# Chunked attention feeding a mixer: undivided groups from the third batch's attention on, held sums, and earlier copies of q

## The chip, the cores and the metric

The kernel runs on one core of a Trainium2 chip. The metric is the device time of one execution in microseconds (us). The five engines of a core are called here TensorE (PE; its weight loads are PEld), VectorE (DVE), ScalarE (ACT), GpSimd (POOL) and SyncE (SP), which only issues DMAs.

## The reference

Two stages. The first is attention over chunks: 4 batches, 8 heads, 768 positions of 64 numbers. For each chunk of 32 queries the keys are 8 memory keys, 16 positions to the left, the chunk and 8 to the right.

```python
for c in range(nc):
    q_c = q[:, :, c_start:c_end]
    k_full = np.concatenate([mem_k, k[:, :, l_start:r_end]], axis=2)
    v_full = np.concatenate([mem_v, v[:, :, l_start:r_end]], axis=2)
    scores = scale * np.matmul(q_c, k_full.transpose(0, 1, 3, 2))
    a = np.exp(scores - np.max(scores, axis=-1, keepdims=True))
    a = a / (np.sum(a, axis=-1, keepdims=True) + 1e-09)
    out[:, :, c_start:c_end] = np.matmul(a, v_full)
```

The second stage takes the result, 768 positions of 512 numbers for each batch, as x and mixes it:

```python
h = x.transpose(0, 2, 1) @ U @ V
u = x + h.transpose(0, 2, 1)
out = u + np.maximum(u @ w_ch1, 0.0) @ w_ch2      # 512 -> 2048 -> 512
```

All is float32 (U, V and the weights arrive as 64-bit numbers and are decoded on the chip). A number is split into a high and a low part, and each product is made of three matmuls (high by high, high by low, low by high).

## The kernel before, in words

**Stages.** Attention of batch 0 comes first (to about 49 us). Then the mixer's matmuls go batch by batch, and the attention of batch b + 1 is laid piece by piece between the matmuls of batch b. Batch 0's matmuls run to about 214 us, with batch 1's attention from about 122 us; batch 1's to about 372, with batch 2's attention; batch 2's to about 528, with batch 3's attention; batch 3's to the end, alone.

**The mixer.** 768 positions are two blocks of 384. In batch 0 the two blocks are computed plainly (`w1_step`, `w2_step`). From batch 1 on `fast` multiplies both blocks and pairs of hidden tiles at once with seven products in place of eight: `fold_both` makes seven sums of transposed u (`th`, `tl`, high and low part), `prepare` makes five sums of weight tiles of a pair on GpSimd, and `build_factor` splits them into high and low on ScalarE (cast) and VectorE (subtraction). `products(p)` runs the 42 matmuls of pair p into three PSUM banks, `first_block` and `second_block` the second layer.

**Borders.** After the third and the seventh product and after every `w2_step` stands a border (`fast_border`; in batch 0 `border`). There the next item of the attention is written: a turn of k or q (transposes on TensorE, then copies by ScalarE or VectorE), a score part, a turn of the softmax's result, or a weighing part (softmax times v). `PLACES` says at which borders the 20 items stand. The third score part is at border 23, the second weighing at 24.

**Halved groups.** A score part (`s_part`) and a weighing part (`av_part`) have 128 small matmuls each (64 rows by 32 columns, 64 numbers) into two PSUM banks. The first 64 (`half(0)`) are written at the item's border. The second 64, and the softmax or the result's scaling behind them, go into the list `tails`, which is run at the start of the next border.

**Order.** TensorE, GpSimd and SyncE issue in the order in which the program is written, all through. VectorE does so until unit 18 of batch 0 (about 129 us), ScalarE until unit 2. After that a planner orders ScalarE and VectorE from modelled times and priorities; work written under `tc.high_priority(offset=HIGH)` goes ahead of what was written up to 400 steps earlier. PSUM has five banks for the running work (`ps_b`) and three for accumulators (`ps_o`); in SBUF 19 equal slots hold what comes and goes.

**Lines that matter.** L661 score matmuls, L784 weighing matmuls, L681 and L682 maximum and subtraction of the softmax, L582 a turn, L642 the copies of turned q, L600 an edge copy of turned k, L1336 GpSimd's sums, L1417 and L1418 the two steps of `build_factor`, L1379 the fold's sums, L1384 its low parts, L1167 the addition to x, L1206 and L1211 the second layer, L1449 the products. `turned[0][1]` is `tl`; its element (4, 0, last column) is written by the last low part of the last fold.

Of the kernel before, what the change touches and what calls it, by code (L numbers as in the profile page):

```python
# [9 lines left out]
F32 = mybir.dt.float32  # L10
# [26 lines left out]
HIGH = 400  # L37
# [18 lines left out]
def chunk_attn_then_mixer_kernel(  # L56
# [13 lines left out]
    nc = tc.nc  # L70
    ctx.enter_context(tc.manual_schedule(engines={mybir.EngineType.SP}))
    P = 128
# [18 lines left out]
    TOK = TB * P  # L91
# [3 lines left out]
    const = ctx.enter_context(tc.tile_pool(name="const", bufs=1))  # L95
# [73 lines left out]
    for j in range(4):  # L169
        nc.gpsimd.tensor_copy(  # L170
            out=rep[32 * j:32 * j + 32],
            in_=ident[32 * j:32 * j + 32, None, 32 * j:32 * j + 32].broadcast_to([32, 3, 32]),
# [252 lines left out]
    def attention(b, xs):  # L425
# [207 lines left out]
        def q_part(T, h, copy=nc.scalar.copy):  # L633
            psv = turn(qn.pop((T, h)))
            if front[0]:
                qt = home([P, 2, NB, CK], F32, "qt", f"w1_{5 + (2 * T + h) % 3}")
            else:
                qt = slot([P, 2, NB, CK], F32, "qt")
            qts[T, h] = qt
            for q_ in range(2):  # L640
                to, src = qt[:, q_].rearrange("c i (n r) -> c r i n", r=2), psv[:, q_]
                copy(out=to, in_=src)  # L642
# [89 lines left out]
        def s_recip(T):  # L732
# [2 lines left out]
            nc.vector.tensor_scalar_add(out=rs, in0=rs, scalar1=1e-9)  # L735
            nc.vector.reciprocal(out=rs, in_=rs)

        def s_part(T):
            banks, psv, half = s_half(T)

            def others():
                half(1)
                s_weights(T, banks, psv)
                s_sums(T)
                s_recip(T)

            tails.append(others)

        def t_part(T, s):
            pt = pts[T, s]  # L750
# [8 lines left out]
        def av_part(T):  # L759
            psv, half = av_half(T)  # L760

            def others():
                half(1)
                x_part(T, psv)
                issued.add(f"av{T}")

            tails.append(others)

        def av_turn(T):
            psv, half = av_half(T)  # L770
# [195 lines left out]
        else:  # L966
# [27 lines left out]
                part(T, h)  # L994

            def q_shared(T, h):
                q_part(T, h, (nc.scalar.copy, nc.vector.tensor_copy)[h])

            order = (
                (turn_in, (k_part, "kn", 0)), (turn_in, (q_shared, "qn", 0)), (turn_both, (1,)),  # L1000
# [303 lines left out]
    tails = []  # L1304
# [6 lines left out]
    def border():  # L1311
        run_tails()
        place(PLAN[at[0]])
        at[0] += 1

    sums_d = [[dram.tile([P, 2, 2, P], F32, name=f"sumsd{p}_{m}") for m in range(3)] for p in range(NF // 2)]

    def prepare(p, first):

        if first:  # L1320
            whole = [slot([P, NCK, P], F32, "val") for _ in range(2)]
            for side in range(2):
                nc.gpsimd.dma_start(out=whole[side], in_=val_d[2 * p + side])
            mixed[p, 1], mixed[p, 3] = whole[1][:, 2:4, :], whole[0][:, 0:2, :]
        else:
            plain = slot([P, 2, 2, P], F32, "plain")
        for m, (n, fa, ca, fb, cb, op) in enumerate(SUMS):
            if m % 2 == 0:
                two = slot([P, 2, 2, P], F32, "sums")
                used = slice(0, 1 if m + 1 == len(SUMS) else 2)  # L1330
                if not first:
                    nc.sync.dma_start(out=two[:, used], in_=sums_d[p][m // 2][:, used])
            mixed[p, n] = two[:, m % 2]
            if first:
                a, b_ = (whole[f][:, 2 * c:2 * c + 2, :] for f, c in ((fa, ca), (fb, cb)))
                nc.gpsimd.tensor_tensor(out=two[:, m % 2], in0=a, in1=b_, op=getattr(ALU, op))  # L1336
                if m % 2 == 1 or m + 1 == len(SUMS):
                    summed.append((p, sums_d[p][m // 2][:, used], two[:, used]))
            elif m == 0:
                for n, side in ((1, 1), (3, 0)):  # L1340
                    mixed[p, n] = plain[:, side]
                    nc.sync.dma_start(out=plain[:, side], in_=val_d[2 * p + side][:, 2 * side:2 * side + 2])
# [244 lines left out]
```

## Time and profile before

| | |
|---|---|
| time, median of 3 runs | 659.44 us (659.01 to 659.98) |
| profiled execution, its own time | 656.65 us |
| its span, first to last instruction | 654.9 us |
| mean granted clock of TensorE | 0.992 |
| PE | 629.9 us busy (96%), 6198 matmuls |
| PEld | 548.8 us (84%), 6198 weight loads |
| DVE | 419.6 us (64%), 889 instructions |
| ACT | 306.9 us (47%), 770 instructions |
| POOL | 74.2 us (11%), 128 instructions |
| DMA | 96.83 MB in 134357 packets, mean 148 GB/s |

The profile is of one execution. Busy time counts an engine's instructions; a wait is the idle time before an instruction and is put down to what ended it. "issue" means that nothing in the profile ended it. Matmuls are pipelined, so that a busy matmul may be shown longer than the step to the next one. A granted clock of 1.00 is 2.4 GHz, 0.50 is 1.2 GHz.

### The profile page before, as it was taken

Reading aid. Unit: us, or ns where it says so; the run is one execution under the profiler, and the core shown is the slowest. Engines: PE = TensorE matmul, PEld = TensorE weight load, DVE = VectorE, ACT = ScalarE, POOL = GpSimd, SP = SyncE. Lnnn points to the kernel's source line nnn. Section 1 sums busy time; section 2 is a strip of 40 time slices with the busy share of each in tenths; the row PEclk is TensorE's granted clock in tenths of the full one; section 3 lists DMA queues with packets and bytes.
Section 4 is the critical chain, followed back from the end, with each engine's and each line's share of the span. In section 5 each row is a group of like instructions: output and inputs, shape, how many; then the busy total and the mean of one; then the engine's idle time right before and its main releaser. Section 6 shows DMA issues by size and latency. Waiting matters only on the chain.

```text
span 654.9 us, 15747 instructions
## 1 busy us (share of the span) xinstructions
PE 629.9 (96%) x6198; PEld 548.8 (84%) x6198; DVE 419.6 (64%) x889; ACT 306.9 (47%) x770; POOL 74.2 (11%) x128
## 2 busy tenths in 40 slices
PE   8788999999999899998999999998999999999997
PEld 6667999978878898777898899877979899989986
DVE  4877997886539756347576863655756975427442
ACT  4566676585226455324334555632433643315321
POOL 3610011100112630123300000000000000000000
PEclk9899999999999999998999999999999999999999
DMA  8797685695606888133361689143422673101022
GB/s 209 180 302 285 216 268 167 195 272 138 186 18 217 226 211 239 33 99 108 104 233 49 170 206 235 34 114 107 130 86 92 206 237 97 49 6 43 2 70 76
DMA packets 134357, 96.83 MB, mean 148 GB/s; under 512 B 88842, under 2 KB 111114, under 8 KB 134282
## 3 DMA queue, kind: packets, MB, share of 16 engines
q1 hardware_dynamic: 121690, 70.25, 38.8%
q10 hardware_dynamic: 9936, 17.04, 7.0%
q0 software_dynamic: 2656, 8.52, 3.9%
q8 instruction: 49, 0.80, 0.5%
q14 instruction: 26, 0.21, 0.1%
HBM read 69.44 MB, written 25.43 MB: 145 GB/s over the span
## 4 chain that ended last, share of the span: by engine, by line
PE 88%; DMA 5%; DVE 3%; SPq 1%; issue 1%; ACT 1%; DVEq 0%; ACTq 0%
PE ps_h L1449 20%; PE acc L1206 14%; PE ps_h L1152 9%; PE ps_a L1449 8%; PE acc L1211 7%; PE ps_h L1206 6%; PE ps_a L1206 5%; PE ps_h L1211 3%; PE ps_a L582 2%; PE ps_a L1211 2%; PE ps_a L784 2%; DMA rw<-in_moe_w_ch_dram 2%; PE ps_a L661 2%; DMA vb<-in_v_dram 2%; PE ps_a L754 1%; PE ps_h L1198 1%
## 5 line engine op out<-in xcount | busy, mean ns | idle before, releaser
L1206 PE MATMUL acc<-w,hh 128*128 128x512 f32 x366 | 97.5, 401 | 1.0 <-DVE w L367 1.0
L1449 PE MATMUL ps_h<-th,w1l 128*128 128x384 f32 x288 | 84.5, 345 | 0.0
L1206 PEld LDWEIGHTS acc<-w,hh 128*128 128x128 f32 x366 | 66.7, 188 | 15.4 <-issue 1.5
L1425 DVE SCALAR_TENSOR_TENSOR hl<-kept,hh 128x384 fp32r<-128x384 f32 x48 | 26.9, 561 | 55.4 <-PE ps_a L1211 29.0
L1424 ACT ACTIVATE hh<-kept 128x384 fp32r<-128x384 f32 x48 | 25.4, 530 | 67.1 <-PE ps_a L1206 42.6
L1449 PEld LDWEIGHTS ps_h<-th,w1l 128*128 128x128 f32 x288 | 53.4, 190 | 3.2 <-issue 1.7
L1449 PE MATMUL ps_h<-th,s 128*128 128x384 f32 x192 | 52.9, 336 | 0.0
L1211 PE MATMUL acc<-w,hl 128*128 128x512 f32 x183 | 51.7, 390 | 0.0
L1449 PE MATMUL ps_h<-tl,w1l 128*128 128x384 f32 x144 | 48.9, 340 | 1.2 <-DVE tl L1384 1.2
L1206 PE MATMUL ps_h<-w,hh 128*128 128x512 f32 x156 | 43.5, 401 | 0.0
L1152 PE MATMUL ps_h<-uh,w1h 128*128 128x384 f32 x124 | 42.2, 346 | 0.8 <-ACT uh L1124 0.8
L1152 PE MATMUL ps_h<-ul,w1h 128*128 128x384 f32 x124 | 40.8, 337 | 0.0
L1211 PEld LDWEIGHTS acc<-w,hl 128*128 128x128 f32 x183 | 34.4, 188 | 7.5
L1206 PE MATMUL ps_a<-w,hh 128*128 128x512 f32 x132 | 37.9, 390 | 1.8 <-ACT hh L1158 1.8
L1455 ACT COPY part<-ps_h 128x384 f32<-128x384 f32 x24 | 11.5, 480 | 58.5 <-PE ps_h L1449 48.0
L1457 DVE TENSOR_TENSOR part<-ps_a,part 128x384 f32<-128x384 f32 x24 | 13.3, 556 | 35.8 <-PE ps_a L1449 34.6
L1417 ACT CAST s<-sums 128x256 fp32r<-128x256 f32 x72 | 28.6, 412 | 15.2 <-PE ps_h L1449 15.2
L1449 PEld LDWEIGHTS ps_h<-th,s 128*128 128x128 f32 x192 | 35.1, 188 | 0.0
L1336 POOL TENSOR_TENSOR sums<-val 128x256 f32<-128x256 f32 x40 | 31.5, 812 | 25.2 <-DMA val<-vald 14.2
L1206 PEld LDWEIGHTS ps_h<-w,hh 128*128 128x128 f32 x156 | 28.1, 188 | 5.7
L1418 DVE TENSOR_TENSOR w1l<-sums,w1l 128x256 fp32r<-128x256 f32 x48 | 21.2, 442 | 18.0 <-ACT w1l L1417 17.8
L1449 PE MATMUL ps_h<-tl,s 128*128 128x384 f32 x96 | 32.3, 336 | 0.0
(279 smaller groups left out, 1414.5 us busy)
## 6 DMA issues: line engine op xcount, KB each, us to landing
sums<-sumsd SPq DMA_DIRECT2D x32, 256.0 KB
xd<-x ACTq DMA_DIRECT2D x30, 256.0 KB
x<-xd SPq DMA_DIRECT2D x30, 256.0 KB
rw<-in_moe_w_ch_dram SPq DMA_DIRECT2D x14, 512.0 KB
vb<-in_v_dram SPq DMA_DIRECT2D x56, 98.0 KB
raw<-in_moe_w_ch_dram SPq DMA_DIRECT2D x20, 256.0 KB
qn<-in_q_dram SPq DMA_DIRECT2D x36, 128.0 KB
rw<-in_moe_w_ch_dram SPq DMA_DIRECT2D x16, 256.0 KB
```

Source lines behind the costliest of these rows:

```text
L582: nc.tensor.transpose(out=psv[:, p, r, :], in_=half[:, r, 2 * p:2 * p + 2, :].rearrange("n h d -> n (h d)"), identity=ident,)
L661: nc.tensor.matmul(out=psv[s][CK * i:CK * i + CK, t, p % 2, p // 2, :], lhsT=qt[p // 2][rows, p % 2, NI * t + i, :], rhs=kall[rows, NB * ( ...
L1152: nc.tensor.matmul(out=ph[:, :TOK], lhsT=w[:, c, :], rhs=u[c], start=(m == 0), stop=(m + 1 == len(parts)),)
L1206: nc.tensor.matmul(out=acc[tt], lhsT=h[:, sl], rhs=w, start=(begins and m == 0), stop=False,)
L1211: nc.tensor.matmul(out=acc[tt], lhsT=hl[:, sl], rhs=w2h[f], start=False, stop=ends is not None)
L1336: nc.gpsimd.tensor_tensor(out=two[:, m % 2], in0=a, in1=b_, op=getattr(ALU, op))
L1417: nc.scalar.copy(out=s[:, 0:2], in_=total)
L1418: nc.vector.tensor_tensor(out=s[:, 2:4], in0=total, in1=s[:, 0:2].bitcast(F32), op=ALU.subtract)
L1424: nc.scalar.activation(out=hh, in_=src, func=AF.Relu)
L1425: nc.vector.scalar_tensor_tensor(out=hl, in0=src, scalar=0.0, in1=hh.bitcast(F32), op0=ALU.max, op1=ALU.subtract,)
L1449: nc.tensor.matmul(out=banks[at_], lhsT=w[:, wc, :], rhs=t[:, i, c, :], start=(n < 3 and m == 0), stop=(m + 1 == len(parts)), skip_group_c ...
L1457: nc.vector.tensor_tensor(out=ta, in0=b2, in1=ta, op=ALU.subtract)
```

## The change

Three edits.

1. A score part and a weighing part hand their second half to a new function, `put_off`. While batch 1's attention is written it goes into `tails` as before. For batches 2 and 3 it is run at once, so that all 128 matmuls, and the softmax or the scaling, are written at the item's own border. (Batch 0's attention does not use these functions.) "Batch 0" in the change's own name is the batch whose matmuls run beside batch 1's attention.
2. The copies of the first turned q of batch 1 (`q_shared`: two on ScalarE, two on VectorE) are written with priority.
3. GpSimd copies one number out of `tl` into a new one-column tile ahead of its five sums for the second pair of batch 1. The number is written by the last low part of the last fold, and GpSimd issues in order, so these sums, and all that is written behind them on GpSimd, come after that fold.

```diff
+        def put_off(others):
+            if b == 1:
+                tails.append(others)
+            else:
+                others()
+
         def s_part(T):
             banks, psv, half = s_half(T)
...
                 s_sums(T)
                 s_recip(T)
 
-            tails.append(others)
+            put_off(others)
...
                 x_part(T, psv)
                 issued.add(f"av{T}")
 
-            tails.append(others)
+            put_off(others)
...
             def q_shared(T, h):
-                q_part(T, h, (nc.scalar.copy, nc.vector.tensor_copy)[h])
+                with tc.high_priority(offset=HIGH):
+                    q_part(T, h, (nc.scalar.copy, nc.vector.tensor_copy)[h])
...
+    gate_ = const.tile([P, 1], F32, name="gate")
...
             mixed[p, 1], mixed[p, 3] = whole[1][:, 2:4, :], whole[0][:, 0:2, :]
+            if p == 1:
+                nc.gpsimd.tensor_copy(out=gate_[0:1], in_=turned[0][1][0:1, 4, 0, TOK - 1:TOK].bitcast(F32))
```

## Rows read from the trace of the kernel before

**Rows 1.** TensorE's waits, whole span: who waited for whom, total us, times, longest.

```profile
PE ps_a L784 <- DVE pt L682: 5.3, 4, 2.4
PE ps_a L661 <- issue: 3.9, 3, 1.7
```

**Rows 2.** Timeline, TensorE, batch 1: start us, us, instruction, idle before, releaser.

```profile
292.54 0.86 PE L661 MATMUL ps_a<-kall,qt 64*32 64x64 f32 x64
...
296.67 0.86 PE L661 MATMUL ps_a<-kall,qt 64*32 64x64 f32 x64
...
299.90 0.27 PE L784 MATMUL ps_a<-vb,pT 64*32 64x64 f32 x2 [2.37 <-DVE pt L682]
```

**Rows 3.** Timeline of the same stretch, VectorE.

```profile
297.91 1.29 DVE L681 TENSOR_REDUCE mx<-ps_a 128x8 f32<-128x512 f32 x2
299.12 1.28 DVE L682 TENSOR_TENSOR pt<-ps_a,mx 128x512 f32<-128x512 f32 x2
```

**Rows 4.** Timeline, TensorE, batch 2, the same place.

```profile
455.36 0.27 PE L784 MATMUL ps_a<-vb,pT 64*32 64x64 f32 x2 [2.32 <-DVE pt L682]
```

**Rows 5.** Three stretches: busy us of PE, PEld, DVE, ACT, POOL, granted clock, DMA.

```profile
293.40:296.70 3.30, 3.30 (x24) 3.05 (x24) 1.19 (x3) 1.19 (x3) 0.56 (x1) 1.00 0.66 250
301.20:304.60 3.40, 3.40 (x23) 3.35 (x11) 1.28 (x4) 0.78 (x2) 2.79 (x4) 0.50 0.02 5
456.70:460.10 3.40, 3.40 (x27) 3.38 (x20) 1.80 (x5) 1.57 (x4) 0.00 (x0) 1.00 0.02 5
```

**Rows 6.** Timeline, TensorE: an undivided group of the opening, a half group.

```profile
36.54 1.48 PE L784 MATMUL ps_a<-vbe,pt 64*32 64x64 f32 x128
...
271.18 0.86 PE L784 MATMUL ps_a<-vb,pT 64*32 64x64 f32 x64
```

**Rows 7.** Timeline, TensorE, second score part of batch 1's matmuls.

```profile
277.37 0.86 PE L661 MATMUL ps_a<-kall,qt 64*32 64x64 f32 x64
...
280.45 0.76 PE L661 MATMUL ps_a<-kall,qt 64*32 64x64 f32 x52
281.98 0.33 PE L661 MATMUL ps_a<-kall,qt 64*32 64x64 f32 x12 [0.77 <-issue]
```

**Rows 8.** The page's DMA queues: packets, MB, share of 16 engines.

```profile
q8 instruction: 49, 0.80, 0.5%
```

**Rows 9.** DMA packets that began from 279.4 to 279.6 us: packets, MB, share.

```profile
q8 instruction: 1, 0.02, 33.8%
```

**Rows 10.** Timeline, TensorE and ScalarE, first score part of batch 1's attention.

```profile
133.59 1.03 PE L582 MATMUL ps_a<-ident,qn 128*128 128x128 f32 x8
...
138.23 0.26 ACT L600 COPY kall<-ps_a 128x48 f32<-128x48 f32 x1
...
140.52 0.74 ACT L642 COPY qt<-ps_a 128x256 f32<-128x256 f32 x2
...
141.07 0.96 PE L661 MATMUL ps_a<-kall,qt 64*32 64x64 f32 x64 [1.37 <-issue]
```

**Rows 11.** Timeline, GpSimd, around the last fold.

```profile
209.06 4.30 POOL L1336 TENSOR_TENSOR sums<-val 128x256 f32<-128x256 f32 x5 [3.05 <-DVE tl L1384]
...
222.30 0.73 POOL L590 COPY kall<-memkT 128x256 f32<-128x256 f32 x2
```

**Rows 12.** Line 1418 from 190 to 240: duration ns minimum/median/maximum, starts.

```profile
L1418 DVE TENSOR_TENSOR s<-sums,s x9: 418/421/965, 210.0 to 236.4; 128x256 fp32r<-128x256 f32 x9
```

**Rows 13.** Timeline, VectorE, around the last fold.

```profile
210.03 2.73 DVE L1418 TENSOR_TENSOR s<-sums,s 128x256 fp32r<-128x256 f32 x3
212.68 1.73 DVE L1379 TENSOR_TENSOR fold<-ps_a,fold 128x256 f32<-128x256 f32 x5
...
215.28 1.27 DVE L1167 TENSOR_TENSOR x<-acc,x 128x512 f32<-128x512 f32 x2
```

**Rows 14.** Timeline, TensorE, start of batch 1's products.

```profile
215.07 0.44 PE L1449 MATMUL ps_h<-tl,w1l 128*128 128x384 f32 x1 [1.22 <-DVE tl L1384]
...
217.20 0.45 PE L1449 MATMUL ps_a<-tl,w1l 128*128 128x384 f32 x1 [0.82 <-DVE tl L1384]
```

## The prediction

> **What bounds the kernel now.** I read the busy table first: TensorE is busy for 629.9 of 654.9 us, VectorE for 419.6, so time is won only where TensorE waits or runs at the lower clock. The waits of TensorE over the whole span [rows 1] say where: 5.3 us in four waits of the weighing matmuls (L784) for the softmax subtraction (L682), 3.9 us in three waits of the score matmuls (L661) that are put down to "issue". The timeline places them. In batch 1's matmuls [rows 2] the last group of scores starts at 296.67 and the weighing starts at 299.90 after 2.37 us of idleness. VectorE then shows why [rows 3]: the weighing needs two PSUM banks out of five, three are held by the running products, and the other two hold the third part's scores, whose maxima start only at 297.91 and whose subtractions start at 299.12. They start so late because the second half of these scores is written one border later than the first, just ahead of the weighing. Batch 2 has the same picture [rows 4]. In the first of the two places the granted clock is then 0.50 (1.2 GHz instead of 2.4) for 3.4 us; after the second it stays at 1.00 [rows 5].
>
> **Edit 1: groups in one piece from batch 2's attention on.** It runs within the matmuls of batches 1 and 2, with three score and three weighing parts each: 12 merges. Four terms.
>
> *Bank waits.* The third part's scores are now whole at the border before, and from the end of their first half (292.54 + 0.86) to the group at 296.67 TensorE has 3.3 us of product matmuls [rows 2] ahead of the weighing. The four waits, of which 2.37 and 2.32 are the long ones, are 5.3 us [rows 1, 2, 4]. What is late next is VectorE: two maxima (1.29) and two subtractions (1.28) must end in these 3.3 us [rows 3], and 1.2 us of operations with priority in that stretch [rows 5] go in between: 2.6 + 1.2 = 3.8, so 0.5 us of waiting is left in each place, 0.7 with the steps from one operation to the next: gain 5.3 - 1.4 = 3.9. Bounds 2.0 (VectorE takes all in another order) and 5.3.
>
> *Clock.* The 3.4 us at half rate cost 1.7 us of work; 11 weight loads were done where the other stretch did 20 [rows 5]. They followed the 2.37 us stop. Gain 1.7, bounds 0 and 1.7: the same stop in batch 2 brought no drop, so a shorter one should not, but a new stop elsewhere may.
>
> *Fewer group edges.* A half group of 64 matmuls shows 0.86 us busy, the unhalved group of 128 in the opening 1.48 [rows 6]. A merge saves 2 x 0.86 - 1.48 = 0.24 us, 12 of them 2.9. Bounds 0 and 4.0 (a third of a microsecond each, with the gap at the second group's edge).
>
> *Code loading.* This speaks against the edit. In batch 1 a half group stops after 52 of its 64 matmuls for 0.77 us and no semaphore ends it [rows 7]. One DMA queue carries 49 packets of instructions, 0.80 MB, which is 16 KB a packet [rows 8]; TensorE's 6198 matmuls and 6198 weight loads divided by 49 are 253 instructions a packet, so about 256. A packet began between 279.4 and 279.6 [rows 9], and the stopped group went on at 281.98: some 2.5 us from a packet's start to its use. So a packet's 256 instructions must last as long as its successor's start is late plus 2.5 us. Ordinary matmuls last far longer (49 packets over a span of 654.9 us are 13 us each); an unhalved group has exactly 256 instructions and uses them up in 1.4 to 1.5 us [rows 6]. What counts is where the packet limits fall. I count TensorE's instructions from the limit at 281.98, in steps of 256, along the order after the change. The limit before it lies 250 earlier (104 in the tail, 18 of the step between, 128 in the head), just ahead of the second part's scores at 277.37 [rows 7]: now the whole group lies inside one packet, which lasts 0.5 + 1.4 = 1.9 us. The packet started at least 279.4 - 277.4 = 2.0 us late (the many small loads of v run then), so the stop would be 2.0 + 2.5 - 1.9 = 2.6; I take 2.5. In batch 2 the limit falls about 9 instructions into the same group, the packet lasts 2.3, and with 1 us of lateness the stop is 1.2; I take 1.1. For the first part's scores in batch 1 the limit lies 11 instructions in, the packet lasts 2.4, and I take 0.4. The other nine groups are cut nearer their middles and cost nothing. New stops 4.0, the old 0.77 goes: loss 3.2, bounds a gain of 0.8 and a loss of 15 (lateness 3 at every limit).
>
> The Trainium skill ("Runtime: NRT & Kernel Launch", section on instruction fetch mechanics) says that crossing such a 16 KiB limit costs little and is mostly hidden, since engines dispatch more slowly than code is filled in. By that rule this term would be a gain of 0.8 instead of a loss of 3.2, and the sum would be 4.0 us better; the stop in the row speaks against it for small matmuls.
>
> Edit 1 in sum: 3.9 + 1.7 + 2.9 - 3.2 = 5.3 us.
>
> **Edit 2: priority for the first turned q.** TensorE is done at 139.7 and starts the first scores of batch 1 at 141.07, 1.37 us idle; ScalarE's two copies of q start at 140.52, behind the copies of the second k part and four decoding steps, though q was turned by 134.6 [rows 10]. With priority the two copies (0.74 us) run some 5 us earlier. What is late next is the last edge copy of k at 138.23, done before TensorE comes. So the idle time goes: 1.3, bounds 0 (the copies stay where they are) and 1.4. The 0.74 us are moved, not added; the decoding steps behind them come up to 0.7 later, and TensorE waits for none of them from 142 to 215.
>
> **Edit 3: GpSimd's sums of the second pair.** These five sums run from 209.06 to 213.36 [rows 11], beside VectorE's three subtractions for the first pair's factors, which take 2.73 us there [rows 13] and 0.42 each at the median [rows 12]: 1.47 lost. Behind them the last fold starts at 212.68 [rows 13], and the products wait for its results, 1.22 and 0.82 us [rows 14]. With the sums held, all this starts 1.4 us earlier; the first wait, which ends at 215.07, would end at 213.6, when TensorE is just coming to it (213.85), so it goes. The second result stands behind the two additions to x, 1.27 us from 215.28 on [rows 13]; they too can start 1.3 us earlier, and TensorE goes on at 215.9 instead of 217.20. Gain 1.3; bounds 2.4 (it goes ahead of the additions) and a loss of 1.0. Behind the waiting copy on GpSimd's queue stand the five sums, the clearing of v's edge, two loads and the sums of the third pair, and the copies into kall at 222.30 [rows 11]: all move about 7 us back. The second pair is needed when its products start, near 222; the last low part lands about 216.4, and at 0.86 us a sum [rows 11] the first is ready near 217.5 and the last at 221, and that one is used 4 us into the products. The third pair is needed near 236, with its sums done by about 229.5 instead of 222.3. No load of SyncE's queue waits for these in that time. So the delay costs nothing unless a factor's cast on ScalarE, placed too early, blocks the queue: hence the loss bound.
>
> **Sum.** 5.3 + 1.3 + 1.3 = 7.9 us. On the profiled execution (656.65, span 654.9) that makes 648.75, span 647.0. The three timed runs have a median of 659.44, 2.8 above the profiled one; off that, 651.5.
>
> **Rivals.**
> A. Code limits cost nothing, and the 0.77 had another cause. For it: of the 24 half groups of batches 1 and 2 only one stops so [rows 1, 7]. Against it: the packet that began 2.5 us ahead of the restart. Time: 651.5 - 3.2 - 0.8 = 647.5. (It is the rule of the page named above.)
> B. Edits 2 and 3 change nothing, because the order on ScalarE and VectorE is planned from modelled times and the copies and the fold keep their places. For it: the additions were planned ahead of the fold's second result [rows 13]. Time: 651.5 + 2.6 = 654.1.
> C. Code lateness of 2 us at every limit: by the same count the first and second score parts then stop 2.5 and 2.6 in batch 1, 1.3 and 2.3 in batch 2, two other groups 0.3 together, 9.0 instead of 4.0, and a stop of 2.6 us brings a clock drop like that at 301.2, 1.7. Time: 651.5 + 5.0 + 1.7 = 658.2, about no change.
> D. Slower: the same mechanism at a lateness of 3 us, as it would be if the small loads of v, which now start one border earlier, sit in front of the code. Then those four stop 1 us longer each (12.7) and four others 3.1 together, 15.8 us in all, plus a drop: 651.5 + 11.8 + 1.7 = 665.0. It decides from a lateness of about 2.4 us. For it: rows 7 and 9 give 2.0 in just that stretch. Against it: other limits outside that stretch do not stop even now.
>
> **How the numbers follow.** Forecast 0.55, A 0.14, B 0.13, C 0.11, D 0.07. The forecast's own range is 648.5 to 654.5. A measurement here can tell about 0.2%, 1.3 us, from no change. Faster by more than that (under 658.1) are the forecast, A, B and half of C, less some 0.03 for an unlucky planned order: 0.84. Within: half of C and that rest, 0.08. Slower: D and a little, 0.08. Range 645.5 to 658.0: below it lies only the case that all gains reach their upper bound (5.3 + 1.7 + 4.0 + 0.8 + 1.4 + 2.4 = 15.6, which is 643.8), above it D and half of C.
>
> **What would show it.** Right: no wait of L784 for L682 over 1 us; groups of 128 small matmuls from 249 to 475; the clock at 1.00 around 300; the first scores of batch 1 with no idle time before them; the second pair's sums after the last fold's results, VectorE's factor subtractions at 0.42 each, and the products' waits under 1.2 us together. The code term shows as stops inside the second part's scores, about 2.5 us in batch 1 and 1.1 in batch 2, with "issue" beside them. Wrong: stops in more than four of the groups, a clock drop behind them, or a new wait of TensorE for factors of the second or third pair.

## The result and the profile after

The changed kernel takes 648.05 us (median of 4 runs, 647.76 to 649.22) where the kernel before took 659.23 in the same comparison (4 runs, 656.45 to 659.98): ratio 0.9841, 95% interval 0.9810 to 0.9872. The forecast was 651.5 in a range of 645.5 to 658.0. The profiled execution after has a time of its own of 647.76 and a span of 646.0 us, 8.9 less than before; the sum of the prediction was 7.9. The result is 3.5 us below the forecast; 1.0 of this lies in the profiled executions, the other 2.5 in the medians, which are 2.6 above the profiled execution before and 0.3 above it after.

One statement ahead of the prediction was wrong: the element (4, 0, last column) of `tl`, which holds GpSimd's sums back, is written by the second of the last fold's four low parts as VectorE runs them, not by the last. From the weighing matmuls on, the lines of code stand 6 to 10 further on than before: L784 is L790, L1206 is L1213, L1384 is L1394, L1336 is L1346, L1418 is L1428, L1449 is L1459.

Three of the lines of TensorE's waits of after, as [rows 1] (who waited for whom, total us, times, longest):

```profile
PE ps_h L1213 <- issue: 1.8, 1, 1.8
...
PE ps_a L661 <- issue: 1.4, 2, 1.1
...
PE ps_a L1459 <- DVE tl L1394: 1.0, 1, 1.0
```

No wait of L790 for the softmax (L682) is listed any more; a new one at the top, 1.8 us of L1213 put down to "issue", has come. The timeline of TensorE in batch 1's matmuls, to be laid beside [rows 2] and [rows 7]:

```profile
274.47 1.48 PE L661 MATMUL ps_a<-kall,qt 64*32 64x64 f32 x128
...
277.74 1.20 PE L1213 MATMUL ps_h<-w,hh 128*128 128x512 f32 x4 [1.78 <-issue]
...
291.57 1.48 PE L661 MATMUL ps_a<-kall,qt 64*32 64x64 f32 x128
...
296.31 1.48 PE L790 MATMUL ps_a<-vb,pT 64*32 64x64 f32 x128
```

The third part's 128 scores are one row at 291.57, the weighing at 296.31 has no bracket, so it starts behind the matmul ahead of it. VectorE in the same place, as [rows 3]:

```profile
293.31 1.29 DVE L681 TENSOR_REDUCE mx<-ps_a 128x8 f32<-128x512 f32 x2
...
294.52 1.28 DVE L682 TENSOR_TENSOR pt<-ps_a,mx 128x512 f32<-128x512 f32 x2
```

The subtractions end at 295.80, half a microsecond ahead of the weighing. The second score part, though, is followed by a stop of 1.78 us that no semaphore ends, and the clock falls there instead of at 301. Two stretches, as [rows 5] (busy us of PE, PEld, DVE, ACT, POOL, granted clock, DMA):

```profile
279.10:282.60 3.50, 3.50 (x10) 2.72 (x9) 1.72 (x3) 1.56 (x3) 1.75 (x3) 0.51 0.03 8
300.50:303.90 3.40, 2.93 (x20) 2.65 (x19) 3.40 (x11) 1.85 (x5) 2.01 (x4) 1.00 0.18 61
```

In the second stretch VectorE is busy throughout and TensorE idle for 0.47 us. This is a wait that the kernel before has not, of the products for one of VectorE's sums:

```profile
303.50 0.44 PE L1459 MATMUL ps_h<-th,w1l 128*128 128x384 f32 x1 [0.47 <-DVE part L1474]
```

The first scores of batch 1 still wait, as in [rows 10], and ScalarE's copies of q stand between two decoding steps:

```profile
139.26 0.75 ACT L642 COPY qt<-ps_a 128x256 f32<-128x256 f32 x2
```

```profile
139.83 0.96 PE L661 MATMUL ps_a<-kall,qt 64*32 64x64 f32 x64 [1.07 <-issue]
```

Around the last fold, VectorE, GpSimd and TensorE in turn, as [rows 13], [rows 11] and [rows 14]:

```profile
208.96 1.09 DVE L1428 TENSOR_TENSOR s<-sums,s 128x256 fp32r<-128x256 f32 x3
209.97 1.74 DVE L1389 TENSOR_TENSOR fold<-ps_a,fold 128x256 f32<-128x256 f32 x5
...
213.76 2.23 DVE L1394 TENSOR_TENSOR tl<-fold,th 128x512 fp32r<-128x512 f32 x2
```

```profile
212.71 0.18 POOL L1334 COPY gate<-tl 1x1 f32<-1x1 f32 x1 [7.77 <-DVE tl L1394]
212.89 4.63 POOL L1346 TENSOR_TENSOR sums<-val 128x256 f32<-128x256 f32 x5
```

```profile
214.91 0.44 PE L1459 MATMUL ps_a<-tl,w1l 128*128 128x384 f32 x1 [1.02 <-DVE tl L1394]
```

The three subtractions take 1.09 us, not 2.73, and of the two waits of the products one is left. But the sums now lie beside the last two low parts, which take 2.23.

By stages, from the starts of each batch's first product in the traces: from batch 1's first product to batch 2's 159.10 before and 154.93 after, to batch 3's 153.93 and 149.92, to the end 128.33 and 128.65. So 4.2 and 4.0 us come from the two batches with groups in one piece, and batch 3, which has none, loses 0.3. The other 1.0 lies ahead of batch 1's first product; the opening alone is 1.3 shorter. It varies from execution to execution (the first layer starts between 42.4 and 46.6 us in the traces of all kernels with this opening), so stages are compared and not spans.

### The profile page after: what moved, and what is told of

Its sections match the earlier page's. It is cut to its first block, busy times and chain, and to the rows that moved or that the text cites. A ratio compares the mean times of both kernels' runs of the same rounds, so it can differ in the third digit from the quotient of the medians.

```text
span 646.0 us, 15746 instructions
## 1 busy us (share of the span) xinstructions
PE 626.6 (97%) x6196; PEld 548.8 (85%) x6198; DVE 422.4 (65%) x889; ACT 306.6 (47%) x770; POOL 75.0 (12%) x129
## 4 chain that ended last, share of the span: by engine, by line
PE 88%; DVE 4%; SPq 2%; ACT 2%; DMA 2%; issue 1%; DVEq 0%; ACTq 0%
PE ps_h L1459 19%; PE acc L1213 14%; PE ps_h L1159 10%; PE ps_a L1459 8%; PE acc L1218 7%; PE ps_h L1213 6%; PE ps_a L1213 5%; PE ps_h L1218 3%; PE ps_a L582 2%; PE ps_a L1218 2%; PE ps_a L790 2%; PE ps_a L661 2%; PE ps_h L1205 1%; PE ps_a L760 1%; PE ps_a L1379 1%
## 5 line engine op out<-in xcount | busy, mean ns | idle before, releaser
L1213 PE MATMUL acc<-w,hh 128*128 128x512 f32 x366 | 97.1, 400 | 0.9 <-DVE w L367 0.9
L1459 PE MATMUL ps_h<-th,w1l 128*128 128x384 f32 x288 | 83.3, 342 | 0.5 <-DVE part L1474 0.5
L1213 PEld LDWEIGHTS acc<-w,hh 128*128 128x128 f32 x366 | 66.9, 188 | 15.2 <-issue 1.5
L1459 PEld LDWEIGHTS ps_h<-th,w1l 128*128 128x128 f32 x288 | 52.8, 187 | 3.7 <-issue 1.7
L1459 PE MATMUL ps_h<-th,s 128*128 128x384 f32 x192 | 53.0, 337 | 0.0
L1459 PE MATMUL ps_h<-tl,w1l 128*128 128x384 f32 x144 | 48.5, 337 | 0.0
L1213 PE MATMUL ps_h<-w,hh 128*128 128x512 f32 x156 | 43.9, 404 | 1.8 <-issue 1.8
L1213 PE MATMUL ps_a<-w,hh 128*128 128x512 f32 x132 | 38.1, 392 | 1.7 <-ACT hh L1165 1.7
L1213 PEld LDWEIGHTS ps_h<-w,hh 128*128 128x128 f32 x156 | 29.0, 192 | 7.8 <-issue 1.9
L1459 PEld LDWEIGHTS ps_h<-th,s 128*128 128x128 f32 x192 | 35.1, 188 | 0.2 <-DVE part L1469 0.2
L1346 POOL TENSOR_TENSOR sums<-val 128x256 f32<-128x256 f32 x40 | 31.9, 825 | 28.1 <-DMA val<-vald 11.0
L1459 PE MATMUL ps_h<-tl,s 128*128 128x384 f32 x96 | 32.3, 337 | 0.0
L1213 PEld LDWEIGHTS ps_a<-w,hh 128*128 128x128 f32 x132 | 25.0, 190 | 7.5 <-ACT hh L1165 2.2
L1428 DVE TENSOR_TENSOR s<-sums,s 128x256 fp32r<-128x256 f32 x72 | 30.4, 434 | 1.0 <-ACT s L1427 0.8
```

The source lines that it names most:

```text
L1213: nc.tensor.matmul(out=acc[tt], lhsT=h[:, sl], rhs=w, start=(begins and m == 0), stop=False,)
L1428: nc.vector.tensor_tensor(out=s[:, 2:4], in0=total, in1=s[:, 0:2].bitcast(F32), op=ALU.subtract)
L1459: nc.tensor.matmul(out=banks[at_], lhsT=w[:, wc, :], rhs=t[:, i, c, :], start=(n < 3 and m == 0), stop=(m + 1 == len(parts)), skip_group_c ...
```

## The experiments

Twelve kernels ran. The table has the ratio to the kernel before (95% interval), the time from batch 1's first product to the end in the trace (441.4 before), and of this what stands between the fourth and the fifth pair's first products of batch 1, where the second score part lies, above the least seen. This excess is a stop and a clock drop if there was one; in two kernels, marked *, 0.65 of it is something else (below, at edit 3).

| kernel | ratio | to the end | of it, above the least |
|---|---|---|---|
| changed kernel | 0.9841 (0.9810 to 0.9872) | 433.5 | 3.46 |
| edit 1 alone | 0.9827 (0.9792 to 0.9862) | 432.0 | 1.99* |
| edit 2 alone | 1.0002 (0.9975 to 1.0028) | 441.9 | |
| edit 3 alone | 1.0016 (0.9987 to 1.0045) | 442.1 | |
| changed kernel again | 0.9845 (0.9807 to 0.9883) | 431.1 | 1.15 |
| gate of 64 bytes | 0.9889 (0.9849 to 0.9929) | 431.5 | 0.99 |
| code limits moved | 0.9908 (0.9872 to 0.9944) | 429.3 | 0.00 |
| second scores halved | 0.9839 (0.9808 to 0.9870) | 429.9 | 0.57, no stop |
| q in a spare tile | 0.9838 (0.9802 to 0.9874) | 430.0 | 0.00 |
| that, and gate without a shift | 0.9773 (0.9741 to 0.9805) | 429.9 | 1.09 |
| that, gate at the third low part | 0.9775 (0.9740 to 0.9810) | 430.0 | 1.18* |
| undivided everywhere | 0.9833 (0.9795 to 0.9870) | 429.7 | 1.77 |
| edit 1 and q in a spare tile | 0.9848 (0.9816 to 0.9880) | 433.2 | 1.24 |

**Each edit alone, and the change again.** Edit 1 alone is the kernel before with one function and two calls changed:

```diff
+        def put_off(others):
+            if b == 1:
+                tails.append(others)
+            else:
+                others()
-            tails.append(others)
+            put_off(others)
```

> Edit 1 alone (undivided groups for batches 2 and 3; no priority for q, no held sums). Theory of separate effects: the four waits of the weighing for the softmax (5.3 us) and the clock drop at 301 (1.7) go, 12 merges give 2.9, the old stop of 0.77 goes; against it the new stop behind the second score part of batch 1 (1.8) with its clock drop (1.7) and 0.7 of small new waits: 6.5 us faster than before, 652 to 653 where before is 659. The idle time before the first scores of batch 1's attention stays 1.4, VectorE's three factor subtractions near 209 stay at 2.7. Rival, the edits only gain together: under 4 us faster.

Edit 2 alone:

```diff
-                q_part(T, h, (nc.scalar.copy, nc.vector.tensor_copy)[h])
+                with tc.high_priority(offset=HIGH):
+                    q_part(T, h, (nc.scalar.copy, nc.vector.tensor_copy)[h])
```

> Edit 2 alone (priority for the first turned q). Theory that something other than priority holds the copies back: they move ahead of one decoding step only, the idle time before the first scores goes from 1.37 to 1.07, 0.3 us faster, not to be told from none. Rival, priority works and the wait moved to something else in the changed kernel: the wait is gone here, 1.3 us faster.

Edit 3 alone:

```diff
+    gate_ = const.tile([P, 1], F32, name="gate")
+            if p == 1:
+                nc.gpsimd.tensor_copy(out=gate_[0:1], in_=turned[0][1][0:1, 4, 0, TOK - 1:TOK].bitcast(F32))
```

> Edit 3 alone (second pair's sums held). Theory: VectorE's three factor subtractions take 1.1 instead of 2.7 us, the products' waits for the fold go from 2.04 to about 1.0, and 1.0 to 1.3 us are gained. Rival, the delay of GpSimd's queue costs as much later: within 0.3 us of before, with a wait of TensorE for a factor of the second or third pair.

The changed kernel again, with nothing edited, for a second trace:

> All three edits, the changed kernel itself, on the same chip as the three single ones. If the edits are separate, its gain is the sum of the three single gains, about 8 us and at most 10.5; if they need each other, it is over 1.5 us more than the sum.

Measured: edit 1 alone has the whole gain, 646.62 against 657.77, 11.2 us where 6.5 were expected; edits 2 and 3 alone cannot be told from no change. By medians the three single gains add up to 9.9 us, and all three edits together gained 10.4 beside them, so the edits do not need each other. Of the twelve kernels only those with edit 2 alone and edit 3 alone, which leave the groups halved, still have the bank waits (5.4 and 5.2 us) and a clock drop at 301 or 302 (3.4 us long, with edit 3 alone 6.8). From batch 1's first product on edit 1 takes 9.3 us off. Its batch 3 is that of before to 0.01. Edit 3 alone makes batch 1's first pair 1.17 shorter (1.36 in the changed kernel, against edit 1 alone), and lengthens three other stretches: from the last pair of batch 1 to batch 2's first and the same one batch later by 0.24 each, and from the last pair to the end by 0.3. In the first two only one kind of instruction is slower, and it makes up 0.24 of the third. The second layer's matmuls with `w2last`, the part of its weights that stays in SBUF: first edit 1 alone, then the changed kernel (minimum/median/maximum ns, starts, form):

```profile
L1204 PE MATMUL acc<-w2last,hh x18: 389/389/389, 347.8 to 625.5; 128*128 128x512 f32 x18
L1204 PE MATMUL ps_h<-w2last,hh x12: 389/389/389, 366.8 to 641.1; 128*128 128x512 f32 x12
```

```profile
L1205 PE MATMUL acc<-w2last,hh x18: 395/396/396, 346.2 to 625.1; 128*128 128x512 f32 x18
L1205 PE MATMUL ps_h<-w2last,hh x12: 395/396/396, 365.3 to 640.9; 128*128 128x512 f32 x12
```

The reader sees 7 ns a matmul, everywhere alike. The gate's tile has one column, but moves all tiles behind it by 32 bytes, `hh` among them, while `w2last` ahead of it stays where it was.

**Four kernels on the changed one.** A gate's tile that takes 64 bytes:

```diff
-    gate_ = const.tile([P, 1], F32, name="gate")
+    gate_ = const.tile([P, 16], F32, name="gate")
```

> All three edits, but the new tile that GpSimd's waiting copy writes is 16 columns (64 bytes) wide instead of one, which with the padding of tiles is 64 bytes instead of 32; every engine issues the same instructions in the same order as in the changed kernel. In the changed kernel hh, hl and most second-layer weights lie 32 bytes further than before while the last weight tile (w2last) stays, and its second-layer matmuls step 7 ns longer each. Theory that the addresses do it: the stretch from the last pair's products of a batch to the next batch's first (1.7 to 2.0, 2.7 to 3.0) is 0.24 us shorter than in the changed kernel, as before, and so is the last batch's end, 0.7 in all. Rival, the three edits' order does it: it stays 0.24 longer each.

Code limits moved, by 20 more of the opening's matmuls that keep the clock up:

```diff
-START = 90
+START = 110
```

> All three edits, with 20 more warm-up matmuls at the very start (110 for 90), which puts 40 instructions ahead of all else on TensorE. Theory of the packet limits: the limit that lay 5 instructions ahead of batch 1's second score part now lies 45 ahead, so 45 ordinary instructions share its packet, which lasts about 5 us instead of 1.9: the stop with 'issue' behind that group (1.8 and 1.1 us in two profiles) goes, and no other group of 128 stops over 0.3. Rival, the small loads of v or a missing buffer stop TensorE there: the stop stays at 1.0 to 1.8.

The second score part halved again, for batch 2's attention alone (the call is `put_off(others, b == 2 and T == 1)`):

```diff
-            if b == 1:
+            if b == 1 or halved:
```

> All three edits, but the second score part of batch 2's attention is halved again (it runs among batch 1's matmuls). Theory of the packet limits: between the same two limits now lies a step of ordinary matmuls, so the packet lasts 3.3 us instead of 1.9, and the stop of 1.1 to 1.8 shrinks by 1.4 to between 0 and 0.8; one more group edge costs 0.3. Net 0 to 1 us faster than the changed kernel. Rival, something else stops TensorE there: a stop of over 1 us stays.

The first q of batch 1 in a tile outside the 19 slots:

```diff
-                qt = slot([P, 2, NB, CK], F32, "qt")
+                qt = (spare if b == 1 and T == 0 else slot)([P, 2, NB, CK], F32, "qt")
```

> All three edits, but the first turned q of batch 1 goes into a spare raw-weight buffer instead of one of the 19 common slots. Theory that the priority was idle because the copies wait for a slot that an x store still reads: the copies on ScalarE now come ahead of the second k part's copies, and the idle time before the first scores (1.07 and 1.09 us in the changed kernel's two profiles, 1.37 before) goes to under 0.2. Rival, the copies wait for TensorE's turn or the scores wait for k: the idle time stays at 1.0.

*Gate.* 64 bytes don't mend it: the three stretches are 0.36, 0.36 and 0.30 longer than in edit 1 alone. `w2last`'s matmuls take 394 ns at the median, and some 6 ns a step are lost in part of the product matmuls too. The thought that tiles need only start at a multiple of 64 fell.

*Limits.* With 40 instructions more ahead of it the second score part has no stop, as the count of 256 instructions has it, although the packet comes late here too: the limit ahead of the group is passed at 278.64 by the count, the packet begins at 279.84, and the 256 instructions last until 284.16. This kernel has the shortest way from batch 1's first product to the end, 429.3. It is no gain in all, since its opening ends later (the first layer starts at 50.1 us in the profiled execution). The limits of the opening have moved too, and one of them now falls into a whole weighing group there, which stops for 3.1 us with a clock drop behind it:

```profile
42.04 0.40 PE L790 MATMUL ps_a<-vbe,pt 64*32 64x64 f32 x2 [3.10 <-issue]
```

So the expectation that no other group stops over 0.3 us failed.

*Halves.* Halved, the second score part of batch 1 has no stop, and costs 0.57 in its place. It also changes VectorE's planned order in batch 2: 0.65 us that the changed kernel loses there (below) are not lost here.

*q.* The wait is gone, so what kept the copies back is the slot that q is written into, one of the 19. In the changed kernel they stand behind three of the four decoding steps that were ahead of them before, and ScalarE is busy up to them. With another tile they start at 136.42, ahead of the edge copies of k; ScalarE and TensorE in this kernel:

```profile
136.42 0.76 ACT L642 COPY qt<-ps_a 128x256 f32<-128x256 f32 x2
```

```profile
139.36 0.84 PE L661 MATMUL ps_a<-kall,qt 64*32 64x64 f32 x63
```

That is worth 1.07, too little for whole times here to show. It needs no priority: in edit 1 with q in the spare tile (below) the copies start at 137.68, and the scores follow without idle time. That a store which still reads the slot is what holds it, as was expected, no row shows.

The same trace has no stop behind the second score part, though the group and the matmuls ahead of it are the changed kernel's:

```profile
273.79 1.48 PE L661 MATMUL ps_a<-kall,qt 64*32 64x64 f32 x128
```

The instruction packets show why. In the changed kernel's trace the limit before the group is passed at 274.48 by the count, with the first of the group's instructions; the packet for the next 256 began between 275.10 and 275.25, and TensorE went on at 277.74, 2.6 us after. In this trace that limit falls four instructions ahead of the group, since TensorE issues four semaphore instructions more before it. It is passed at 273.02, but the packet had begun between 272.05 and 272.20, ahead of it; the next limit is reached at 275.00, 2.9 us after, and nothing waits. The DMA row for each of the two (packets, MB, share), in this order:

```profile
q8 instruction: 1, 0.02, 40.5%
```

```profile
q8 instruction: 1, 0.02, 57.4%
```

The four instructions are not what decides. In the trace of the gate without a shift (below) the limits fall at the same instructions as in this one, but the packet begins at 272.81, 0.6 behind the limit at 272.18, and the group stops where the limit lies, two matmuls before its end:

```profile
275.19 0.30 PE L662 MATMUL ps_a<-kall,qt 64*32 64x64 f32 x2 [0.77 <-issue]
```

Counted in this way, semaphore instructions included, the fourteen traces (with the kernel before) agree: 30 waits of TensorE of 0.3 us and more are put down to "issue", the one ahead of batch 1's first scores left out. All lie at a multiple of 256 instructions from one another, to within the few records that are missing, and end 2.3 to 3.2 us after the start of a packet.

**Four that put these together.** All have the first q of batch 1 in the spare tile. The gate without a shift, in rows that `v3` leaves unused:

```diff
-    v3 = const.tile([96, S], F32R, name="v3")
+    v3all = const.tile([P, S], F32R, name="v3")
+    v3 = v3all[0:96]
-    gate_ = const.tile([P, 1], F32, name="gate")
+    gate_ = v3all[96:97, 0:1]
```

> All three edits, the first q of batch 1 in a spare tile, and the gate's one element kept in rows that the tile v3 leaves unused, so that no tile of the kernel lies elsewhere than in the kernel before. Theory (the 32 bytes by which the gate moved the tiles behind it are what the second layer's matmuls with the kept w2 paid for): the stretches from the last pair of batch 1 and of batch 2 to the next batch's first pair, and from the last pair to the end, are each 0.24 us shorter than with the gate as a tile, 0.7 in all, and the first pair of batch 1 stays 1.4 shorter than with edit 1 alone; span 641.2 if TensorE's code does not stop behind the second score part of batch 1, up to 644.7 if it does. Rival (the order of work or the transfers that the held sums change cost them): the three stretches keep their 0.24. The 0.65 in batch 2's fourth pair stays in both.

That, with the gate at an element of the third low part:

```diff
-turned[0][1][0:1, 4, 0, TOK - 1:TOK]
+turned[0][1][0:1, 3, 1, TOK - 1:TOK]
```

> As the run with the gate in unused rows, but the gate reads an element that the third low part of the last fold writes, not the second. If GpSimd's sums beside the low parts are what is left of the wait at the first products (1.02 us for a low part, two low parts in 2.23 where undisturbed they take 1.28), the third and fourth low parts come at 0.64 each again, the wait falls to about 0.5 and the first pair of batch 1 is 0.4 to 0.6 us shorter; the sums, 1.2 us later, still end before VectorE asks for them at 220.6. Rival: the sums come too late for the second pair, and its first products wait by 0.5 to 1.2 us. A second rival: the wait is set by something else than the port and stays at 1.0.

The gate without a shift, and no group halved in batch 1's attention either:

```diff
-            if b == 1:
-                tails.append(others)
-            else:
-                others()
+            others()
```

> As the run with the gate in unused rows, and no group of 128 small matmuls is halved any more, in batch 1's attention (139 to 185 us) as well. Theory (a halved group costs a second entry of about 0.25 us): six halves fewer make the stretch from batch 1's first scores to its first products 1.5 us shorter (72.5 before this, 71.0 now). Rival: the groups use up TensorE's code faster than it comes; by counting 256 instructions to a packet only the second weighing of those at 175 us has too little time, a stop of up to 2.5 us, with a clock drop of 1.7 behind it at worst, so that the stretch is as long as before or up to 2.7 longer. Bank waits as in the kernel before (5.3) would make it longer still, if banks are lent out there as they were in batch 0.

Edit 1 with q in the spare tile (the diff above), without edits 2 and 3:

> Edit 1 with the first q of batch 1 in a spare tile, without edits 2 and 3. The wait before batch 1's first scores (1.1 to 1.4 us) is gone; batch 1's first pair is 1.4 longer than with the held sums; no 0.24 at the three borders, no 0.65 in batch 2. If the held sums give back as much as they bring, its span from batch 1's first products to the end (432.0 with edit 1 alone, with a stop of 2.0 in it) is within 0.3 us of that of the kernel with all edits and the gate as a tile when neither has a stop (430.0); the kernel with the gate in unused rows should be 0.7 shorter than that.

*Gate without a shift* is the best kernel: 643.44 us (642.14 to 644.91) against 658.64, ratio 0.9773, its interval below that of the changed kernel. `w2last` is back at 389 ns,

```profile
L1206 PE MATMUL acc<-w2last,hh x18: 389/389/389, 342.1 to 620.3; 128*128 128x512 f32 x18
```

and the three stretches equal those of edit 1 alone to 0.01: it was the place in SBUF. The 0.65 in batch 2's fourth pair stays, as both theories had it. Batch 1's first pair is 0.44 shorter still than with q in a spare tile alone, which no theory had. GpSimd's sums and VectorE's low parts beside them, first in the changed kernel, then here:

```profile
L1346 POOL TENSOR_TENSOR sums<-val x5: 720/969/1186, 212.9 to 216.6; 128x256 f32<-128x256 f32 x5
```

```profile
L1394 DVE TENSOR_TENSOR tl<-fold,th x2: 1098/1155/1212, 213.8 to 214.8; 128x512 fp32r<-128x512 f32 x2
```

```profile
L1347 POOL TENSOR_TENSOR sums<-val x5: 734/919/1890, 211.8 to 216.0; 128x256 f32<-128x256 f32 x5
```

```profile
L1395 DVE TENSOR_TENSOR tl<-fold,th x2: 680/681/682, 212.5 to 213.1; 128x512 fp32r<-128x512 f32 x2
```

Here one sum takes 1.89 us and the low parts 0.68 each; there the low parts take 1.1 and 1.2 and no sum above 1.19. Which of the two engines is held back decides, and TensorE waits 0.70 instead of 1.02:

```profile
213.26 0.44 PE L1460 MATMUL ps_a<-tl,w1l 128*128 128x384 f32 x1 [0.70 <-DVE tl L1395]
```

*Gate at the third low part* has undisturbed low parts too and the same wait, 0.70, above the 0.5 expected, so what is left of the wait is not GpSimd's doing; its later sums cost 0.4 in the second pair. No difference in the whole time (643.24).

*Undivided everywhere* is the rival's case. From batch 1's first scores to its first products it takes 75.9 us, where gate without a shift takes 72.3. The second weighing of batch 1, the one named, stops:

```profile
182.13 0.32 PE L788 MATMUL ps_a<-vb,pT 64*32 64x64 f32 x10 [3.97 <-issue]
```

By the count its limit before was passed at 175.09; the packet began only between 179.70 and 179.85, and TensorE went on 2.3 to 2.4 us later. A drop of the clock to 0.51 follows:

```profile
182.60:186.10 3.50, 3.50 (x9) 2.61 (x9) 1.32 (x4) 0.00 (x0) 0.83 (x2) 0.51 0.03 5
```

Stop 4.0 and drop 1.7 less the 3.6 that it is longer leaves 2.0 gained by six merges, 0.34 each; bank waits did not come. In all 0.9833, by median 3.6 us slower than the gate without a shift.

*Edit 1 and q in a spare tile* is slower than expected: the products wait 1.53 and 0.81 us for low parts, and a clock drop follows the second. That pair is 3.4 us longer than with sums held and no shift, 1.7 of it the drop. Less drop and stop its way to the end is 430.2, as expected without them. So without edit 3 the start of the products can cost more than its waits; edit 2 alone has such a drop there too, the kernel before and edit 1 alone, with waits of 2.0 and 2.3 us in all, have none.

What the traces name between the changed kernel and the best one is some 2 us (1.1 for q, 0.7 for the shift, 0.4 for the low parts), and the stops vary by more; the ratios of the two differ by 0.7%, some 4.5 us. Whole runs without a trace can't be taken apart, so the rest stays open.

## Why the prediction came out right, step by step

| step | forecast | measured |
|---|---|---|
| bank waits | +3.9 | +5.3, less a new wait of 0.2 to 0.5 in batch 1 |
| clock | +1.7 | +1.7, the drop at 301 is gone |
| 12 merges | +2.9 | +4.1 to 4.6 |
| code loading | -3.2 | -2.7 in the trace after, a new drop included; +0.2 to -1.0 in others with a stop, +0.8 without one |
| edit 2 | +1.3 | +0.3 |
| edit 3 | +1.3 | +1.4, less 0.7 and at times 0.65 given back |

**Bank waits.** Right in mechanism, too small in size. I left 0.7 us of waiting in each place because 1.2 us of work with priority goes between VectorE's four operations. It does not stand there after: the maxima start 0.3 us after the group's end (291.57 + 1.48) and the four operations take 2.5 us. All 5.3 us went. What is left of VectorE's lateness shows one border further on, as the wait of 0.47 us at 303.50; the traces of batch 2 have none.

**Clock.** The drop at 301 went with its stop. In the changed kernel's trace one of the same length came behind the code's stop; in the second trace of the same kernel, behind a stop of 1.06 us, none. Stops of 1.8, 2.4 and 4.0 have a drop behind them, one of 2.3 in batch 2 has not [rows 5]. The prediction had named a drop behind a code stop as a sign that it was wrong; in the changed kernel's trace it came.

**Merges.** A merge was costed by the busy time of the groups (0.24). What it saves is read from border to border: two halves stand between starts of ordinary matmuls 1.11 and 1.06 us apart, a whole group 1.73, so 0.44. Batch 2 has no stop and no drop, so it checks this: 153.93 before and 148.98 with edit 1 alone, 4.95 less, of which 2.65 are its bank waits; 2.3 are left for six merges, 0.38 each. With undivided groups in batch 1's attention as well a merge came to 0.34. The surplus of this term and of the bank waits covers what edits 2 and 3 did not bring.

**Code loading.** The place was right: the second score part of batch 1, at a packet limit that the count gave, and in no group where the limit cuts it near its middle. What failed are two sizes. The limit falls on the group's first instruction and not some 5 ahead, since TensorE issues five semaphore instructions fewer in the changed kernel, so the packet lasts 1.5 us and not 1.9. And the lateness does not carry over from the kernel before. I took 2.0 us in batch 1 and 1 in batch 2 as fixed; in the kernels without edit 1 the packet begins 1.5 to 2.9 us behind the limit, in those with it from 0.9 ahead to 1.2 behind. For the changed kernel 0.7 of lateness, 2.6 from start to use, less 1.5, is the stop of 1.8 (2.5 forecast). In all TensorE stops for 0 to 1.8 us there. Why the packet comes at a different time is open. In batch 2 (1.1 forecast) the packet begins 0.8 ahead of the limit in the changed kernel, and no run with edit 1 has a stop; the 0.4 of the first part showed in two traces, as 0.37 each (edit 1 alone, and the gate at the third low part). The mechanism is shown by the kernel with moved limits, which takes the stop away here and puts one into the opening, and by the group named in advance, 3.97 us at a lateness of 4.6.

The trace of before held more evidence than I used. The longest of its three waits of scores for "issue" [rows 1] is in the opening, where groups are whole:

```profile
14.94 1.51 PE L661 MATMUL ps_a<-kall,qt 64*32 64x64 f32 x83
18.19 0.94 PE L661 MATMUL ps_a<-kall,qt 64*32 64x64 f32 x45 [1.74 <-issue]
```

It lies at such a limit, and a packet began 2.7 us ahead of its end. What spoke for rival A, that only one of 24 half groups stops, left this one out.

The Trainium skill ("Runtime: NRT & Kernel Launch", section on instruction fetch mechanics) says that the fetch of the next 16 KiB of code is hidden, because instructions are dispatched more slowly than code arrives. Here that holds at nearly every limit, but not where a burst of small matmuls uses up most of a packet: eight of the traces with edit 1 stop behind the second score part, for 0.4 to 1.8 us.

**Edit 2.** The step "with priority the two copies run some 5 us earlier" failed. They start at 139.26 instead of 140.52, in an execution whose opening was 1.3 us ahead, and the wait falls from 1.37 to 1.07. Priority moved them ahead of one decoding step alone; the tile kept them from more, as the kernel with another tile shows. In the one trace of edit 1 alone the wait is 2.67, but by whole times that kernel is not the slower one (646.62 against 647.42), so a larger worth of priority is not shown.

**Edit 3.** Right where I looked: the fold starts earlier, one of the two waits is gone and the pair is 1.4 shorter. I had both the element and the place of the sums wrong: they lie beside the last two low parts, not behind them. What I did not see is outside the stretch: 7 ns for each matmul with `w2last`, 0.72 in all. The 0.65 in batch 2 is another thing: VectorE's row sums (L728) are put ahead of an addition (L1467) that the products need, and

```profile
406.45 0.44 PE L1459 MATMUL ps_a<-th,s 128*128 128x384 f32 x1 [0.23 <-DVE part L1467]
```

is the mark of it. In batch 2 it is in five of the kernels that have edit 1, one of them without held sums, and absent in five, four of them with. Two of these, edit 1 alone and the gate at the third low part, have it in batch 1's fourth pair instead, with a wait of 0.23 and 0.25 as its mark. No kernel without edit 1 has it; among those with it, it goes with the planned order and not with held sums.

**Rivals.** A (limits cost nothing) gave 647.5, nearest to the result, and is false: the stop is there. B is nearly true, edits 2 and 3 bring nothing by whole times, but its 654.1 is not, since edit 1 is larger than its forecast. C and D asked for a lateness of 2 to 3 us at every limit. One limit with 4.6 was seen, in another kernel, none in this one; why it was so late is open. Two opposite errors, edit 1 too small and edits 2 and 3 too large, make the sum look better than its terms.

## What to carry to other kernels

Cost a group of small matmuls from the start of the matmul ahead to the start of the one behind, not by its busy time. Before a new small tile goes into SBUF, look at what it moves: unused rows of a tile that is already there cost nothing. Where a burst uses up 256 instructions in two or three microseconds, count where the packet limits fall, or halve that one group. Count all of them: limits that are moved away from one burst can fall into another, as they did in the opening here.

## What was not expected of the hardware

A shift by 32 bytes of one operand's tile and not of the other made 128x512 matmuls 396 instead of 389 ns, one by 64 bytes 394; where both had moved together (`w` and `hh`) there was no loss. Why is open; a shift by 256 bytes was not tried.

A VectorE operation with two SBUF inputs and a GpSimd one do not slow each other evenly. In the changed kernel they take turns: the low parts take 1.10 and 1.21 us where undisturbed ones take 0.68, and two sums 1.17 and 1.19 against 0.73. In the kernel without a shift one sum waits out both low parts (1.89) and these lose nothing. The Trainium skill ("SBUF — State Buffer", section "SBUF: two separate sides") describes it as an exclusive lock that the first comer keeps for its whole instruction. The changed kernel's trace agrees: the sum that starts at 213.59 takes its 0.72, and the low part that starts at 213.76 ends 0.55 behind it. In the other trace sum and low part start within 0.01 us of each other, and the rows can't tell which came first; a few tens of ns may decide who is held back, which is not shown.
